# Transposing tiles 4 to 7 on VectorE instead of TensorE, spreading the scales of four tiles by one product, and one more gate and up piece ahead of the third attention unit

## The chip, the cores and the metric

The kernel runs on one core of a Trainium2 chip. A core has TensorE (matrix products, PE in the profile), VectorE (DVE), ScalarE (ACT), GpSimd (POOL) and SyncE (SP), which here only issues the DMAs. Each engine works through its own instructions in the order in which they were written, and waits for others by semaphores. The metric is the device time of one execution in microseconds.

## The reference

```python
xn = layernorm(x)                                 # x: 2048 rows of 640
qkv = xn @ wqkv                                   # 32 heads of 20
# each row attends to 8 rows: itself and those 2, 4, ... 14 rows back
logits = einsum("bhsd,bhswd->bhsw", q, k[idx]) * 20 ** -0.5   # masked where idx < 0
s = einsum("bhsw,bhswd->bhsd", softmax(logits), v[idx]) @ wo
h = (xn @ w_gate) * (xn @ w_up)                   # 640 -> 1536
out = x + s * silu(h @ w_down)                    # 1536 -> 640
```

All is in float32. The kernel writes each factor of a product as a high part (TensorE's rounded format) and a low part (the rest), and computes three products: high by high, high by low and low by high.

## The kernel before, in words

The 2048 rows stand as 16 tiles of 128 rows. Partition p of a tile holds row 16p + j of the sequence; tiles 0 to 7 are the even columns j ("even tiles"), tiles 8 to 15 the odd ones. Rows that attend to one another are of the same parity, so attention runs in units (g, r): six groups g of five or six heads by the two parities r, twelve units in all. Unit u multiplies its eight tiles by the weights of its group (`qkv(u, i)`, 15 products for tile i), ScalarE copies the result into q and kv, and the DMA shifts kv by one partition to fill the front. `attention(u)` is a generator of VectorE steps, which `advance` draws from a list `running` at a pace: each product stage adds to a credit, and each step takes its estimated length from it. So VectorE's attention of one unit is woven by hand into the product stages of the next ones. The kv buffers are two, one for each parity; unit u + 2 writes the one that attention(u) read.

The gate and up products run in pieces: `gate_up(f, ch)` is slice f of twelve slices of the hidden features, by chunk ch of four chunks of four tiles. A piece is a g half and a u half, of 15 products with 512 columns each. ScalarE copies g to gs, and the product hs = u * gs is made by `finish` in one of two ways: while an attention is running, by VectorE, deferred into the following piece or unit; otherwise by a copy on ScalarE and a product on GpSimd, at once. hs is stored to h_scr. From the third unit on, three or four pieces follow each unit (`piece`, the loop at L741); those that are left follow the last unit. Then come the last two slices, the output projection and the down projection with the gate.

Every product needs the normalized rows transposed, as four chunks of four tiles (`xT`, high and low part). This is made in two ways:

- Even tiles (0 to 7) go through TensorE. `norm` takes a tile's statistics on VectorE (`moments`), makes the inverse deviation (`rstd`) and applies shift and scale (L209). `trans` transposes it by five products with the identity (L223); ScalarE copies the high part (L224), VectorE subtracts it from the product for the low part (L225).
- Odd tiles (8 to 15) go through VectorE. Their statistics are taken from a first load of the rows. Then the tile is loaded again (`load_xq`) in another order, in which a 32 by 32 block transpose on VectorE (L253) gives the full transpose. In that order a partition holds pieces of four different rows, so the row's scales are needed in the partitions of other quarters: `spread` makes four products of the scales with selecting matrices `sel` (L240) and ScalarE copies the result (L241). `trans_odd` applies four shifts of 160 columns, transposes, lets ScalarE make the high part (L256), and makes the low part of the tile before (`low_parts`, L258), so that VectorE does not stand for ScalarE.

The first unit and the first slices have no attention to be woven with. Their order is written out from L635 to L710: TensorE does qkv(0, 0) to (0, 3) and the first half of piece (0, 0), the transposes of tiles 4 to 7 around piece (1, 0), qkv(0, 4) and (0, 5), piece (0, 1) with the spread in its middle, qkv(0, 6) and (0, 7), piece (1, 1), the eight qkv of unit 1, pieces (0, 2) to (1, 3), then unit 2.

Of the kernel before, what the change touches and what calls it, by code (L numbers as in the profile page):

```python
# [13 lines left out]
AF = mybir.ActivationFunctionType  # L14
# [20 lines left out]
QB = 32  # L35
NQ = P // QB
QC = D // NQ
# [13 lines left out]
def kernel(  # L51
# [11 lines left out]
    nc = tc.nc  # L63
# [66 lines left out]
    xt = {}  # L130
# [14 lines left out]
    xc = st([P, NE, D], "xc", NCH)  # L145
# [6 lines left out]
    ident = st([P, P], "ident", 1)  # L152
# [27 lines left out]
    def moments(s0, n, mv=None):  # L180
        stats = st([P, n, 2, 6], "stats", 2)
        mv = st([P, n, 2], "mv", 2) if mv is None else mv
        for i in range(n):
            for a in range(2):
                nc.vector.bn_stats(stats[:, i, a, :], xt[s0 + i][:, a * HALF:(a + 1) * HALF])
            nc.vector.bn_aggr(mv[:, i, :], stats[:, i])
        return mv
# [20 lines left out]
    def apply(y, m, r):  # L208
        nc.vector.tensor_scalar(y, y, m, r, op0=ALU.subtract, op1=ALU.mult)  # L209

    def norm(s0, n, mv=None):
        mv = moments(s0, n) if mv is None else mv
        r = st([P, n], "r", 2)
        rstd(mv[:, :, 1], r, n)
        for i in range(n):
            apply(xt[s0 + i], mv[:, i, 0:1], r[:, i:i + 1])

    def trans(s, bank=("q", 4)):
        hi, lo = xT_tile(s)
        for k0, k1 in ((0, 4), (4, KD)):  # L220
            p = pt([P, k1 - k0, P], *(("q", 4) if k0 else bank))
            for k in range(k0, k1):
                nc.tensor.transpose(p[:, k - k0, :], xt[s][:, k * P:(k + 1) * P], ident)  # L223
            nc.scalar.activation(hi[:, k0:k1, :], p, AF.Copy)  # L224
            nc.vector.tensor_sub(lo[:, k0:k1, :], p, hi[:, k0:k1, :].bitcast(F32))  # L225

    mvo = st([P, NE, 2], "mvo", 1)
    mro = st([P, 2, NE], "mro", 1)  # L230
    mrq = st([P, NQ, 2, NE], "mrq", 1)

    def load_xq(s, n, t):
        nc.sync.dma_start(t, xq[:, s - NE:s - NE + n, :])

    def spread():

        p = pt([P, NQ, 2, NE], "q", 4)
        for a in range(NQ):
            nc.tensor.matmul(p[:, a], sel[:, a], mro, start=True, stop=True)  # L240
        nc.scalar.activation(mrq, p, AF.Copy)  # L241

    halves = []

    def low_parts():
        while halves:
            halves.pop(0)()

    def trans_odd(s):
        for a in range(NQ):  # L250
            apply(xt[s][:, a * QC:(a + 1) * QC], mrq[:, a, 0, s - NE:s - NE + 1], mrq[:, a, 1, s - NE:s - NE + 1])
        y = st([P, KD, P], "ot", 2)
        nc.vector.transpose(y.rearrange("p k (q i) -> p k q i", i=QB),  # L253
                            xt[s].rearrange("p (q k j) -> p k q j", q=NQ, j=QB))
        hi, lo = xT_tile(s)
        nc.scalar.activation(hi, y, AF.Copy)  # L256
        low_parts()
        halves.append(lambda: nc.vector.tensor_sub(lo, y, hi.bitcast(F32)))  # L258


    UN = [(g, r) for g in range(len(GROUPS)) for r in range(DIL)]
# [21 lines left out]
    def qkv(u, i, runs=ALL_RUNS, at=None, act=None):  # L283

        g, r = UN[u]
        c = GROUPS[g] * DH
        p = pt([P, 3 * c], "q", 4)
        t0 = (i % TPC) * P
        for n, (a, b, k) in enumerate(runs):
            if n == at:  # L290
                act()
            nc.tensor.matmul(p, xT[(r * NE + i) // TPC][a][:, k, t0:t0 + P], wq[g][b][:, k], start=n == 0,  # L292
                             stop=n == len(runs) - 1, skip_group_check=act is not None)
        nc.scalar.activation(kv_t[u][:, :, W - 1 + i, :], p[:, c:].rearrange("p (a c) -> p a c", a=2), AF.Copy)  # L294
# [71 lines left out]
    running = []  # L366
# [14 lines left out]
    def gate_up_half(f, ch, n, p, c=slice(0, CH), **parts):  # L381
        mm3(p[:, c], [([t[:, k, n, :] for t in wf[f]], [t[:, k, c] for t in xT[ch]]) for k in range(KD)], **parts)

    def gate_up(f, ch, between=(), amid=(), part=None):
        if part is None:
            pp = [pt([P, CH], "g", 2), pt([P, CH], "u", 2)]
            c = slice(0, CH)
        else:
            pp, c = part, slice(CH // 2, CH)
        gate_up_half(f, ch, 0, pp[0], c)  # L390
        for act in amid:
            act()
        gs = st([P, CH], "gs", 2)
        nc.scalar.activation(gs, pp[0], AF.Copy)  # L394
        for act in between:
            act()
        share = (c.stop - c.start) / CH
        finish_piece()
        advance(PACE * 3.25 * share)
        gate_up_half(f, ch, 1, pp[1], c)  # L400

        def finish():
            hs = st([P, CH], "hs", 2)
            if running:
                nc.vector.tensor_mul(hs, pp[1], gs)  # L405
            else:
                nc.scalar.activation(hs, pp[1], AF.Copy)
                nc.gpsimd.tensor_mul(hs, hs, gs)
# [10 lines left out]
    def finish_piece():  # L419

        while unfinished:
            unfinished.pop(0)()
# [238 lines left out]
    sel = st([P, NQ, P], "sel", 1)  # L661
    nc.gpsimd.tensor_copy(sel.rearrange("p q (b i) -> p q b i", i=QB),
                          ident.rearrange("p (q i) -> p q i", i=QB).unsqueeze(2).to_broadcast([P, NQ, NQ, QB]))
# [8 lines left out]
    moments(10, 2, mvo[:, 2:4])  # L672
    load_xq(8, 4, xc[:, 4:8])
    trans(7)
    load_wf(2)
    qkv(0, 4)
    qkv(0, 5)
    moments(12, 2, mvo[:, 4:6])
    moments(14, 2, mvo[:, 6:8])
    load_xq(12, 3, xa)  # L680
    load_xq(15, 1, xd)
    nc.vector.tensor_copy(mro[:, 0, :], mvo[:, :, 0])
    rstd(mvo[:, :, 1], mro[:, 1, :], NE)
    gate_up(0, 1, amid=(spread,))
    trans_odd(8)
    trans_odd(9)
    qkv(0, 6)
    trans_odd(10)
    qkv(0, 7)
    trans_odd(11)  # L690
    gate_up(1, 1, amid=(lambda: trans_odd(12),))
    trans_odd(13)
    begin_unit(1)
    for i in range(8):
        if i == 3:
            running.append((0, attention(0)))
        if i == 2:
            load_wq(1, ((0, 3), (3, 5)))
            low_parts()
        if i < 2:  # L700
            trans_odd(14 + i)
# [12 lines left out]
    def piece():  # L714
        f, ch = pieces.pop(0)
        if ch == 0:
            load_wf(f + 1)
        gate_up(f, ch, (lambda: split_wf(f + 1, nc.gpsimd),) if ch == 1 else ())
# [19 lines left out]
            split_wq(UN[u + 1][0], nc.gpsimd)  # L738

    f0, f1 = KF - 2, KF - 1  # L740
    for u in range(2, len(UN)):  # L741
        unit(u)
        for _ in range(3 + (u in (2, 5)) if u + 1 < len(UN) else len(pieces)):
            if len(pieces) == 1:
                load_wf(f1)
            piece()
    for ch in range(NCH):
        gate_up(f0, ch)
        if ch == 0:
# [3 lines left out]
            t = load_wo((4,))  # L753
# [49 lines left out]
    for m in range(n_prod):  # L803
        n, j = divmod(m, 7)
# [61 lines left out]
```

## Time and profile before

| | us |
|---|---|
| median of 3 runs | 786.98 (786.91 to 787.13) |
| profiled execution | 786.92 |
| its span, first to last instruction | 785.0 |
| TensorE busy | 777.6 (99%) |
| VectorE busy | 661.4 (84%) |
| ScalarE busy | 234.4 (30%) |
| GpSimd busy | 145.5 (19%) |

A row of the profile's timeline gives the start, the time to the end of the last of a run of equal instructions, engine, line, operation, the tile written and those read, shape and count; in brackets is the idle time of the engine ahead of it and what ended that. Products overlap in the pipe, so a row's end lies behind the start of the next row. A row of the waits names the engine and line that waited, what it waited for, the total, how often, and the longest. Line numbers are those of the kernel before.

### The profile page before, as it was taken

To read this page: it belongs to the slowest core of one execution; us is meant where nothing else is said; L and a number is where in the kernel's file an instruction comes from. 1 tells how busy PE (TensorE), PEld (TensorE's weight loads), DVE (VectorE), ACT (ScalarE), POOL (GpSimd) and SP (SyncE) were. 2 spreads that over 40 slices of the span, in tenths; PEclk is the share of its full clock that TensorE was granted. 3 is DMA by queue.
4 is the path that set the end of the run, shared out by engine and by line. 5 is a ranking of instruction groups with operands and counts; after the bars stand their busy time and mean duration, and the time that the engine had idled before them with its cause. 6 is when DMAs were issued, how large, how long until landed. Compare 5 with 4: busy or idle time off the path is not lost.

```text
span 785.0 us, 11221 instructions
## 1 busy us (share of the span) xinstructions
PE 777.6 (99%) x4454; PEld 709.0 (90%) x4454; DVE 661.4 (84%) x660; ACT 234.4 (30%) x536; POOL 145.5 (19%) x110
## 2 busy tenths in 40 slices
PE   8999999999999999999999999999999999999997
PEld 6889898889898898899898989888899999999997
DVE  6989899999999979997999999991278677777775
ACT  4434211121122211311221212012366564444442
POOL 4401212022023100500231000113467600000000
PEclk9999999999999999999999999999999999999999
DMA  9162122141142221404032132332797574555534
GB/s 326 70 223 86 31 70 63 48 123 48 50 113 80 75 71 61 118 27 112 28 113 77 58 86 59 112 96 66 166 262 222 169 268 139 206 201 181 181 101 135
DMA packets 81661, 92.68 MB, mean 118 GB/s; under 512 B 23032, under 2 KB 63304, under 8 KB 81480
## 3 DMA queue, kind: packets, MB, share of 16 engines
q1 hardware_dynamic: 81608, 91.96, 37.9%
q8 instruction: 35, 0.57, 0.3%
q14 instruction: 18, 0.15, 0.1%
HBM read 54.53 MB, written 28.31 MB: 106 GB/s over the span
## 4 chain that ended last, share of the span: by engine, by line
PE 98%; ACT 1%; DMA 1%; DVE 0%; SPq 0%; issue 0%
PE q L292 27%; PE u L95 21%; PE g L95 21%; PE q L605 11%; PE q L95 9%; PE u L605 5%; PE g L605 3%; DMA wraw<-in_wqkv 1%; PE q L223 0%; ACT wf L85 0%; ACT xc L224 0%; SPq L135 0%; DVE t L209 0%; ACT wqh L85 0%; PE q L240 0%
## 5 line engine op out<-in xcount | busy, mean ns | idle before, releaser
L95 PE MATMUL u<-xc,wf 128*128 128x512 f32 (+1 forms) x735 | 176.2, 391 | 0.0
L95 PE MATMUL g<-xc,wf 128*128 128x512 f32 (+1 forms) x735 | 176.2, 391 | 0.0
L95 PEld LDWEIGHTS u<-xc,wf 128*128 128x128 f32 x735 | 135.9, 188 | 32.1
L95 PEld LDWEIGHTS g<-xc,wf 128*128 128x128 f32 x735 | 135.4, 188 | 30.8
L292 PE MATMUL q<-wqh,xc 128*128 128x300 f32 (+1 forms) x960 | 159.8, 310 | 0.9 <-ACT xc L224 0.9
L292 PEld LDWEIGHTS q<-wqh,xc 128*128 128x128 f32 x960 | 146.1, 188 | 2.9 <-ACT xc L224 1.3
L326 DVE TENSOR_TENSOR t<-q,kv 128x1600 f32<-128x1600 f32 (+1 forms) x48 | 98.8, 2058 | 9.6 <-DMA kv<-kv 9.6
L347 DVE TENSOR_TENSOR t<-e,kv 128x1600 f32<-128x1600 f32 (+1 forms) x48 | 96.9, 2037 | 1.1
L86 POOL TENSOR_TENSOR wf<-wraw,wf 128x256 fp32r<-128x256 f32 (+2 forms) x22 | 47.1, 2161 | 253.0 <-ACT wf L85 253.0
L329 DVE TENSOR_REDUCE lg<-t 128x80 f32<-128x1600 f32 (+1 forms) x48 | 92.6, 1930 | 1.2
L394 ACT ACTIVATE gs<-g 128x512 f32<-128x512 f32 x48 | 28.7, 598 | 205.8 <-PE g L95 197.2
L292 PE MATMUL q<-wql,xc 128*128 128x300 f32 (+1 forms) x480 | 86.3, 310 | 0.0
L355 DVE TENSOR_TENSOR t<-t,t 128x1600 f32<-128x1600 f32 (+1 forms) x36 | 78.6, 2184 | 1.1
L292 PEld LDWEIGHTS q<-wql,xc 128*128 128x128 f32 x480 | 74.4, 188 | 0.0
L294 ACT ACTIVATE kv<-q 128x200 f32<-128x200 f32 (+1 forms) x96 | 33.4, 348 | 135.7 <-PE q L292 135.6
L605 PE MATMUL q<-xc,wf 128*128 128x320 f32 x432 | 67.3, 309 | 0.0
L605 PEld LDWEIGHTS q<-xc,wf 128*128 128x128 f32 x432 | 64.3, 188 | 0.0
L86 POOL TENSOR_TENSOR wql<-wraw,wqh 128x300 fp32r<-128x300 f32 (+4 forms) x15 | 33.2, 2239 | 142.5 <-ACT wqh L85 142.5
L95 PE MATMUL q<-wf,wf 128*128 128x320 f32 x156 | 35.7, 311 | 0.0
L405 DVE TENSOR_TENSOR hs<-u,gs 128x512 f32<-128x512 f32 x39 | 26.6, 683 | 0.8 <-issue 0.8
L86 DVE TENSOR_TENSOR wf<-ot,wf 128x640 fp32r<-128x640 f32 x13 | 17.2, 1322 | 12.0 <-ACT wf L85 12.0
L95 PEld LDWEIGHTS q<-wf,wf 128*128 128x128 f32 x156 | 26.1, 189 | 0.0
(169 smaller groups left out, 890.8 us busy)
## 6 DMA issues: line engine op xcount, KB each, us to landing
h_scr<-hs SPq DMA_DIRECT2D x48, 256.0 KB, 2.3
wraw<-in_wgu SPq DMA_DIRECT2D x12, 640.0 KB, 4.9
t<-h_scr SPq DMA_DIRECT2D x8, 768.0 KB, 7.5
hs<-s_scr SPq DMA_DIRECT2D x16, 320.0 KB, 4.0
gs<-in_x SPq DMA_DIRECT2D x16, 320.0 KB, 4.4
wraw<-h_scr SPq DMA_DIRECT2D x12, 384.0 KB, 5.7
out<-q SPq DMA_DIRECT2D x14, 320.0 KB, 3.6
wraw<-in_wd SPq DMA_DIRECT2D x12, 320.0 KB, 4.9
```

Source lines behind the costliest of these rows:

```text
L86: eng.tensor_sub(lo, raw, hi.bitcast(F32))
L95: nc.tensor.matmul(acc, a, b, start=first and n == 0, stop=last and n == len(runs) - 1)
L292: nc.tensor.matmul(p, xT[(r * NE + i) // TPC][a][:, k, t0:t0 + P], wq[g][b][:, k], start=n == 0, stop=n == len(runs) - 1, skip_group_check ...
L294: nc.scalar.activation(kv_t[u][:, :, W - 1 + i, :], p[:, c:].rearrange("p (a c) -> p a c", a=2), AF.Copy)
L326: nc.vector.tensor_mul(t, q.rearrange("p i c -> p (i c)").unsqueeze(1).to_broadcast([P, 2, NE * c]), places(0, j))
L329: nc.vector.tensor_reduce(out=lg[:, :, j:j + 2].rearrange("p n a -> p a n"), in_=heads(t), op=ALU.add, axis=AX.X)
L347: nc.vector.tensor_mul(heads(t), pw, heads(places(1, j)))
L355: nc.vector.tensor_add(acc, acc, t)
L394: nc.scalar.activation(gs, pp[0], AF.Copy)
L405: nc.vector.tensor_mul(hs, pp[1], gs)
L605: nc.tensor.matmul(p, y[:, i, k], wd_t[name][k][:, l], start=new and r == 0, stop=r == len(runs) - 1, skip_group_check=True)
```

## The change

Tiles 4 to 7 are now treated as the odd tiles are: statistics from the first load, a second load of each tile in the other order, four shifts, the block transpose on VectorE, high part on ScalarE, low part on VectorE. `trans_q` replaces `trans_odd`, and works by groups of four tiles. The host's array xq holds twelve tiles instead of eight. The twenty transposing products of these tiles on TensorE are gone; those of tiles 0 to 3 remain.

`scales(s0)` makes the scales of a group and multiplies them by `quarter`, a matrix of ones and zeros, so that each partition's two numbers per tile stand only in the columns of its own quarter. `spread(s0)` is then one product with one selecting matrix, for each of three groups; before it was four products for all eight odd tiles. GpSimd builds `quarter` and `sel` in ten small steps.

The written order changes with it. qkv(0, 4) to (0, 7) now run in a row behind piece (1, 0). Statistics of tiles 8 to 15 come behind the transposes of 4 to 7. Piece (0, 2) stands in the middle of unit 1, and attention(0) is put on the list behind it and behind the last transpose. Piece (2, 0) runs ahead of unit 2, so two pieces instead of three are left behind the last unit. hs is made by VectorE, deferred, in all pieces but the very last.

```diff
-    def spread():
-        p = pt([P, NQ, 2, NE], "q", 4)
-        for a in range(NQ):
-            nc.tensor.matmul(p[:, a], sel[:, a], mro, start=True, stop=True)
-        nc.scalar.activation(mrq, p, AF.Copy)
+    def scales(s0):
+        mv, mr = stat[s0]
+        nc.vector.tensor_copy(mr[:, 0, :], mv[:, :, 0])
+        rstd(mv[:, :, 1], mr[:, 1, :], TPC)
+        own[s0] = st([P, NQ, 2, TPC], "own", 2)
+        nc.vector.tensor_mul(own[s0], mr.unsqueeze(1).to_broadcast([P, NQ, 2, TPC]),
+                             quarter.unsqueeze(2).unsqueeze(3).to_broadcast([P, NQ, 2, TPC]))
+    def spread(s0):
+        p = pt([P, NQ, 2, TPC], "q", 4)
+        nc.tensor.matmul(p, sel, own[s0], start=True, stop=True)
+        spread_t[s0] = st([P, NQ, 2, TPC], "mrq", 2)
+        nc.scalar.activation(spread_t[s0], p, AF.Copy)
...
+        last = (f, ch) == (KF - 1, NCH - 1)
...
-            if running:
+            if not last:
                 nc.vector.tensor_mul(hs, pp[1], gs)
...
-        if not running:
+        if last:
             finish_piece()
...
-    norm(4, 4)
+    quarter, sel = st([P, NQ], "quarter", 1), st([P, P], "sel", 1)
...
+    for i in range(TPC):
+        moments_q(4 + i, 1)
+        load_xq(4 + i, 1, xc[:, i:i + 1])
+    scales(4)
     qkv(0, 2)
     qkv(0, 3)
     gate_up(0, 0, part=part0)
-    trans(4)
-    trans(5)
-    moments(8, 2, mvo[:, 0:2])
-    gate_up(1, 0, amid=(lambda: trans(6),))
...
+    spread(4)
+    trans_q(4)
+    finish_piece()
+    trans_q(5)
+    gate_up(1, 0)
     load_wf(2)
+    trans_q(6)
+    trans_q(7)
     qkv(0, 4)
     qkv(0, 5)
...
+    low_parts()
+    finish_piece()
+    moments_q(8, 4)
+    load_xq(8, 4, xc[:, 4:8])
+    scales(8)
+    qkv(0, 6)
+    qkv(0, 7)
+    moments_q(12, 4)
     load_xq(12, 3, xa)
     load_xq(15, 1, xd)
...
+    scales(12)
+    gate_up(0, 1, amid=(lambda: spread(8),))
+    trans_q(8)
+    trans_q(9)
+    finish_piece()
+    trans_q(10)
+    gate_up(1, 1, amid=(lambda: spread(12),))
+    trans_q(11)
     begin_unit(1)
+    trans_q(12)
+    finish_piece()
+    for i in range(TPC):
+        if i == 1:
             load_wq(1, ((0, 3), (3, 5)))
+        qkv(1, i)
+    trans_q(13)
+    trans_q(14)
+    gate_up(0, 2)
+    trans_q(15)
+    low_parts()
+    running.append((0, attention(0)))
+    for i in range(TPC, NE):
         qkv(1, i)
         advance(PACE * 1.9)
     running.append((1, attention(1)))
     split_wq(1, nc.gpsimd)
-    gate_up(0, 2)
     gate_up(1, 2)
...
+    piece()
     for u in range(2, len(UN)):
         unit(u)
...
-    odd = arrays["x"].reshape(NQ, QB, NE, DIL, NQ, QC)[:, :, :, 1]
-    arrays["xq"] = lay(odd.transpose(3, 1, 2, 0, 4).reshape(P, NE, D))
+    quarters = arrays["x"].reshape(NQ, QB, NE, DIL, NQ, QC).transpose(3, 4, 1, 2, 0, 5).reshape(DIL, P, NE, D)
+    arrays["xq"] = lay(np.concatenate([quarters[0][:, TPC:], quarters[1]], axis=1))
```

More of the change, by code (lines that the diff above doesn't have):

```diff
@@ L225, in trans, with moments_q, trans_q @@
             nc.vector.tensor_sub(lo[:, k0:k1, :], p, hi[:, k0:k1, :].bitcast(F32))
-    mvo = st([P, NE, 2], "mvo", 1)
-    mro = st([P, 2, NE], "mro", 1)
-    mrq = st([P, NQ, 2, NE], "mrq", 1)
-    def load_xq(s, n, t):
-        nc.sync.dma_start(t, xq[:, s - NE:s - NE + n, :])
-    def spread():
-        p = pt([P, NQ, 2, NE], "q", 4)
-        for a in range(NQ):
[L240 to L249, printed above, removed]
-        for a in range(NQ):
-            apply(xt[s][:, a * QC:(a + 1) * QC], mrq[:, a, 0, s - NE:s - NE + 1], mrq[:, a, 1, s - NE:s - NE + 1])
+    stat = {s: (st([P, TPC, 2], "mvo", 3), st([P, 2, TPC], "mro", 3)) for s in range(TPC, NT, TPC)}
+    own, spread_t = {}, {}
+    def moments_q(s, n):
+        s0 = s // TPC * TPC
+        moments(s, n, stat[s0][0][:, s - s0:s - s0 + n])
+    def load_xq(s, n, t):
+        nc.sync.dma_start(t, xq[:, s - TPC:s - TPC + n, :])
+    def scales(s0):
[10 more added lines that the diff above has]
+        nc.scalar.activation(spread_t[s0], p, AF.Copy)
+    halves = []
+    def trans_q(s):
+        m, i = spread_t[s // TPC * TPC], s % TPC
+        for a in range(NQ):
+            apply(xt[s][:, a * QC:(a + 1) * QC], m[:, a, 0, i:i + 1], m[:, a, 1, i:i + 1])
         y = st([P, KD, P], "ot", 2)
```

37 lines of the change are left out of this document (11 added, 26 removed).

## The prediction

> **What bounds the kernel now.** I read the page's busy shares and its chain first, then who TensorE waited for.
>
> ```profile
> span 785.0 us, 11221 instructions
> ...
> PE 777.6 (99%) x4454; PEld 709.0 (90%) x4454; DVE 661.4 (84%) x660; ACT 234.4 (30%) x536; POOL 145.5 (19%) x110
> ...
> PE 98%; ACT 1%; DMA 1%; DVE 0%; SPq 0%; issue 0%
> ```
> ```profile
> PE q L292 <- ACT xc L224: 0.9, 2, 0.6
> PE q L223 <- PE u L95: 0.4, 1, 0.4
> ```
>
> TensorE is busy 99% of the span, carries 98% of the chain, and behind its first products waits for nothing longer than 0.6 us. So a product taken from it is worth its whole time, as long as no new wait appears, and VectorE, at 84%, is the engine that could bring one. The stage that changes, on TensorE in order of time (start, us, what, count):
>
> ```profile
> 22.93 1.92 PE L95 MATMUL g<-xc,wf 128*128 128x256 f32 x15
> 24.68 1.91 PE L95 MATMUL u<-xc,wf 128*128 128x256 f32 x15
> 26.96 1.30 PE L223 MATMUL q<-ident,xc 128*128 128x128 f32 x10 [0.37 <-PE u L95]
> 28.02 3.75 PE L95 MATMUL g<-xc,wf 128*128 128x512 f32 x15
> 31.61 0.71 PE L223 MATMUL q<-ident,xc 128*128 128x128 f32 x5
> ...
> 36.11 0.94 PE L292 MATMUL q<-wqh,xc 128*128 128x300 f32 x5
> ...
> 43.81 0.96 PE L240 MATMUL q<-mro,sel 128*128 128x16 f32 x8
> 44.62 3.74 PE L95 MATMUL u<-xc,wf 128*128 128x512 f32 x15
> ...
> 59.31 0.86 PE L292 MATMUL q<-wqh,xc 128*128 128x300 f32 x5
> ...
> 75.81 3.66 PE L95 MATMUL g<-xc,wf 128*128 128x512 f32 x15
> 79.30 3.66 PE L95 MATMUL u<-xc,wf 128*128 128x512 f32 x15
> ```
>
> Products overlap, so I count from start to start. From 59.31 to 75.81 run eight products of qkv: 2.06 us each. A half of gate_up (15 products of 512 columns) is 79.30 − 75.81 = 3.49 us, a piece 7.0; a half of 256 columns is 24.68 − 22.93 = 1.75.
>
> **What the change takes from TensorE and gives it.** Before, 36.11 − 24.68 = 11.43 us go from the u half of piece (0, 0) to qkv(0, 4), and hold 1.75 + 7.0 of that half and piece (1, 0). The other 2.68 us are the twenty transposes of tiles 4 to 7 with the 0.37 us wait ahead of them. They go. The spread of the odd tiles is four products; from 36.11 to 59.31 there are 23.20 us, of which 4 × 2.06 and four halves make 22.24, so it costs 0.96. In its place come three spreads of one product each: by a quarter of that row 0.24 each; bounds 0.10 (an eighth of 0.81) and 0.96. I take 0.24, as a product of the same kind.
>
> So TensorE saves 2.68 + 0.96 − 3 × 0.24 = 2.92 us, less the waits it gets anew. These stand in VectorE's queue.
>
> ```profile
> 20.31 0.88 DVE L185 BATCH_NORM_STATS2 stats<-xc 128x6 f32<-128x320 f32 x2
> ...
> 24.44 0.34 DVE L194 TENSOR_SCALAR rstd<-mv 128x4 f32<-128x4 f32 x1
> ...
> 41.90 0.17 DVE L682 COPY mro<-mvo 128x8 f32<-128x8 f32 x1
> ...
> 43.14 0.17 DVE L206 TENSOR_TENSOR mro<-rstd 128x8 f32<-128x8 f32 x1
> ...
> 49.65 1.45 DVE L258 TENSOR_TENSOR xc<-ot,xc 128x640 fp32r<-128x640 f32 x1 [0.44 <-ACT xc L256]
> 51.03 1.17 DVE L209 TENSOR_SCALAR xc<-xc,mrq 128x160 f32<-128x160 f32 x4
> ...
> 53.00 0.78 DVE L258 TENSOR_TENSOR xc<-ot,xc 128x640 fp32r<-128x640 f32 x1
> 53.71 1.17 DVE L209 TENSOR_SCALAR xc<-xc,mrq 128x160 f32<-128x160 f32 x4
> ...
> 68.85 1.82 DVE L326 TENSOR_TENSOR t<-q,kv 128x1600 f32<-128x1600 f32 x1
> ...
> 88.98 0.49 DVE L340 TENSOR_REDUCE sm<-e 128x40 f32<-128x320 f32 x1 [3.35 <-ACT e L338]
> ...
> 104.51 0.68 DVE L405 TENSOR_TENSOR hs<-u,gs 128x512 f32<-128x512 f32 x1
> 105.11 1.81 DVE L355 TENSOR_TENSOR t<-t,t 128x1600 f32<-128x1600 f32 x1
> ```
> ```profile
> 44.80 0.22 ACT L241 ACTIVATE mrq<-q 128x64 f32<-128x64 f32 x1 [2.54 <-PE q L240]
> ...
> 53.12 0.74 ACT L256 ACTIVATE xc<-ot 128x640 fp32r<-128x640 f32 x1 [2.17 <-DVE ot L253]
> ...
> 86.56 0.60 ACT L394 ACTIVATE gs<-g 128x512 f32<-128x512 f32 x1 [6.40 <-PE g L95]
> ...
> 106.06 0.34 ACT L294 ACTIVATE kv<-q 128x200 f32<-128x200 f32 x1 [4.91 <-PE q L292]
> ```
> ```profile
> 25.18 0.60 POOL L662 COPY sel<-ident 128x512 f32<-128x512 f32 x1
> ...
> 49.12 1.30 POOL L408 TENSOR_TENSOR hs<-hs,gs 128x512 f32<-128x512 f32 x1 [11.30 <-ACT hs L407]
> ```
>
> The steps from these rows: statistics of four tiles 24.44 − 20.31 = 4.1; scales of a group 43.14 + 0.17 − 41.90 = 1.4 plus 0.2 for the new product of 32 columns (bounds 0.17 and 0.34, the nearest small rows), so 1.6; shift and transpose of a tile, 53.00 − 51.03 = 1.97; a low part 0.71; ScalarE's high part 0.74 in between; a product hs 105.11 − 104.51 = 0.60.
>
> **The first spread.** VectorE reaches scales(4) at 24.44, as now, and has its operand at about 26.5. GpSimd builds sel in five fills, three sums and a copy instead of one copy, from 25.18: at least 0.8 us (nine times about 0.09), at most 3.5 (each step at 0.60 or less, fills at a tenth). By the columns it is about 1.3, so 26.5. TensorE is free at 24.68 + 1.75 = 26.43. I take the spread at 26.88, a wait of 0.45 (from 0.05 to 2.3, where sel is the last).
>
> **The chain on VectorE.** With the spread's copy on ScalarE (0.22, some 0.3 after the product starts), VectorE starts on tile 4 at 27.6. Its order is: tile 4, hs, tile 5, low 4, tile 6, low 5, tile 7, low 6, low 7, hs, statistics of 8 to 11, scales, statistics of 12 to 15, scales, tiles 8 and 9, low 8, hs, tile 10, low 9, tile 11, low 10, tile 12, low 11. Summed, low 4 ends at 32.85, low 5 at 35.5, low 6 at 38.2, low 7 at 39.0, the scales of 8 at 45.3 and of 12 at 51.1, low 8 at 55.7, low 9 at 59.0, low 10 at 61.7, low 11 at 64.35.
>
> TensorE: spread done 27.12, piece (1, 0) to 34.12, qkv(0, 4) to (0, 7) to 42.36, g of (0, 1) to 45.86, spread(8), u to 49.60, g of (1, 1) to 53.10, spread(12), u to 56.84, then qkv(1, 0) to (1, 3) at 56.84, 58.90, 60.96 and 63.02. A product of qkv reads the low part in its last third, 1.37 us after its start: 58.2, 60.3, 62.3, 64.4. So low 8 has 2.5 us to spare, low 9 1.3, low 10 0.6, and **low 11 nothing**. Each us that VectorE is later from here back to tile 4 is a us of TensorE. I put 0.2 us there.
>
> Sum: 2.92 − 0.45 − 0.2 = 2.27 us.
>
> **What lies beside.** Four hs of this stage and four near the end leave ScalarE and GpSimd for VectorE; three are in the chain (1.8 us). Four reloads of 320 KB, 1.28 MB more to move, go into SP's queue right behind the last first load, each after its tile's statistics (from 21.3), with only the later h_scr stores behind them. SP then holds load_wf(2), two shift DMAs of kv (waiting for qkv(0, 4)), a store, and only then the reload of 8 to 11, which waits for the statistics of tile 11 (43.6), and behind it the second pair of kv shifts.
>
> ```profile
> xc<-in_xq SPq DMA_DIRECT2D x1, 1280.0 KB, 6.8
> t<-in_xq SPq DMA_DIRECT2D x1, 960.0 KB, 9.8
> ```
> ```profile
> DMA  9999999977744310000000000000000000000000
> ```
>
> At 6.8 us it lands at 50.4, wanted at 51.1: covered, by 0.7. The second row is the DMA share from 20 to 27 us in 40 slices: the engines run empty at 22.8, so tile 4's reload, wanted at 27.5, has 6.2 us and a free path.
>
> **Attention and the piece moved ahead.** attention(0) starts at about 73.8 instead of 68.85, five us late. Its exponentials stand on ScalarE behind a gs, now that of (0, 3), whose g ends at 65.08 + 7.0 + 8.25 + 7.0 + 3.5 = 90.8. From the gs at 86.56 to VectorE's next step at 88.98 it was 2.4; so that step now runs at 93.2. Its last read of kv ends where the row at 104.51 begins, so at 108.7. Unit 2 writes the same kv buffer: its first copy ran at 106.06, 1.5 us behind. With piece (2, 0) ahead, TensorE starts unit 2 at 63.02 + 2.06 + 7.0 + 8.25 + 28 = 108.3, and the copy comes at 110.5: 1.8 us to spare, as before. The piece itself costs nothing, being work moved from behind the last unit. Without this cover the copy would wait 5.2 us, which the three further product banks (6.2 us) would just hold. load_wf(3) moves ahead with the piece and waits in SP for GpSimd's low half of wf(2), holding back only stores. At the end, attention(11) finishes later by about five us, against this wait:
>
> ```profile
> DVE ot L466 <- DMA wraw<-o_scr: 20.9, 1, 20.9
> ```
>
> **A rule weighed.** The low part at 49.65 took 1.45, the one at 53.00 0.78; GpSimd's hs product, at 49.12 for 1.30, ends when the first gets going. With the hs products gone from GpSimd, all low parts of the chain should take the short value, which the sum uses. The Trainium skill, "SBUF — State Buffer", section "SBUF: two separate sides", says VectorE and GpSimd share a port pair by an exclusive lock, held for a whole instruction; the trace agrees (0.67 us lost). By that rule, the other side also holds: GpSimd's new small steps and the fill of the second kv buffer now fall on the scales of tile 4 and its first shift.
>
> ```profile
> 61.55 1.26 POOL L278 MEMSET kv<- 1x1400 f32 x1
> ```
>
> **The rivals.**
> 1. *Tiles 8 to 11 land late.* At the 9.8 us of the other reload, 53.4 instead of 51.1: the chain is 2.3 later and so is low 11. 787.0, no change. For it: kv shifts share the path. Against: the neighbours that filled the engines then (load_wf(2), two more reloads) are now earlier or later. 0.13.
> 2. *GpSimd delays the start.* If its fill of 1.26 us holds up tile 4's first shift, the whole chain is 1.26 later, and low 11 with it: 784.65 + 1.26 = 785.9, within 0.2%. For it: the fill stands right behind sel in GpSimd's queue. Against: half of it may be over by 27.6. 0.05. (This is the time by the rule of the section just named.)
> 3. *Slower: VectorE becomes the bound of the stage.* Its 36.8 us from tile 4 to low 11 have no slack, so TensorE pays each us. It decides at 2.27 us (6% of the chain), and costs 0.2% from 3.84; were all eight low parts at 1.45, it would be 8 × 0.67 = 5.4 us: 790.1. For it: the mean share of 84% hides that this stretch is full, and rows beside GpSimd are slow. Against: GpSimd is idle there. 0.10.
> 4. *Slower by the first reload.* Were tile 4's reload as slow as the first loads of single tiles (the row below), it would land at 21.3 + 11.8 = 33.1, the chain 5.6 later: 790.2. Against: the empty engines above. 0.08.
>
> ```profile
> t<-in_x SPq DMA_DIRECT2D x3, 320.0 KB, 11.8
> ```
>
> **The numbers.** The profiled execution took 786.92 us, 1.92 outside its span of 785.0, and the median of the runs is 786.98. 786.92 − 2.27 = 784.65, against the median 784.7. The forecast has the remaining 0.64, its own range 783.6 (first spread without wait, spreads at 0.10) to 785.4. For four in five the range is 783.7 to 787.6, which takes in rivals 1 and 2 and sel as the last, and leaves out 3 and 4. 0.2% of 787 is 1.57 us, about what can be told from no change: faster 0.64, same 0.18, slower 0.18.
>
> **What would show it.** Right: no L223 row on xc; qkv(0, 4) at about 34.1, qkv(1, 0) at 56.8; attention(0) at 73.8 on VectorE; spreads of about 0.24; TensorE's waits up by under 0.7 us. Wrong: a wait of qkv in unit 1 for VectorE's low parts over 1 us, a wait at the first spread for GpSimd, or VectorE waiting for a reload.

## The result and the profile after

| | us |
|---|---|
| median of 22 runs after the change | 785.87 (785.35 to 786.74) |
| median of 22 runs before it | 787.31 (786.82 to 788.47) |
| ratio of after to before | 0.9983, 95% interval 0.9976 to 0.9989 |
| profiled execution after | 786.40, its span 784.6 |

The change saves 1.3 us (0.9 to 1.9), 0.17%. That is in the forecast direction, some 60% of the 2.27 us forecast, and just inside the 0.2% that the prediction called no change. The page of the changed kernel, busy shares and the chain's share by engine:

```profile
PE 776.7 (99%) x4432; PEld 708.3 (90%) x4432; DVE 667.5 (85%) x691; ACT 230.6 (29%) x527; POOL 135.6 (17%) x110
...
PE 96%; DMA 1%; POOL 1%; DVE 1%; SPq 0%; ACT 0%; issue 0%
```

TensorE has 22 instructions fewer and is still the bound. Of its waits behind its first products, the 0.4 us ahead of the transposes are gone, and the changed stage has one new wait, that for `sel` at the first spread:

```profile
PE q L250 <- POOL sel L681: 0.5, 1, 0.5
```

Another new one, of 0.5 us for rows that VectorE normalizes (L209), lies in the start-up at 17.27, ahead of the change. The stage on TensorE (timeline, as in the prediction; the five rows that carry the steps):

```profile
25.51 1.94 PE L95 MATMUL u<-xc,wf 128*128 128x256 f32 x15
27.99 0.41 PE L250 MATMUL q<-own,sel 128*128 128x32 f32 x2 [0.55 <-POOL sel L681]
...
35.31 0.85 PE L304 MATMUL q<-wqh,xc 128*128 128x300 f32 x5
...
58.04 0.85 PE L304 MATMUL q<-wqh,xc 128*128 128x300 f32 x5
...
109.75 0.85 PE L304 MATMUL q<-wqh,xc 128*128 128x300 f32 x5
```

From the u half of piece (0, 0) to qkv(0, 4) it is now 35.31 − 25.51 = 9.80 us (11.43 before), and from there to qkv(1, 0) 58.04 − 35.31 = 22.73 (23.20 before). Together 2.10 us are saved of the 2.47 forecast for these two stretches. Unit 1 and pieces (0, 2) to (1, 3) take 109.75 − 58.04, less 7.0 for the piece ahead, 44.71 us; before, they took 103.97 − 59.48 = 44.49 (first two rows of the next fence). 0.2 us are lost there, and the stage as a whole brings 1.9 us.

More is lost behind the stage, where nothing was changed. Units of the chain (start, us, what), before and then after:

```profile
59.48 16.49 PE q L292 x120
103.97 16.48 PE q L292 x120
...
343.08 19.84 PE q L292 x120
```
```profile
109.91 16.59 PE q L304 x120
...
349.39 19.84 PE q L304 x120
```

A unit of five heads (products of 300 columns) takes 16.59 instead of 16.48 us, 138.25 ns a product instead of 137.3; one of six heads takes 19.84 as before. Eight units of five heads make 8 × 0.11 = 0.9 us, six of them (0.66) behind the stage. 1.9 − 0.66 = 1.2 us, which is the measured gain within its interval. The profiled executions differ by only 786.92 − 786.40 = 0.5 us, because the one of the changed kernel comes to its u half at 25.51 us instead of 24.68. The start-up varies from run to run: the kernel before with its weights moved (an experiment below) comes there at 25.29, and a variant of the changed kernel at 24.82.

VectorE, GpSimd and ScalarE, where the prediction had named moments:

```profile
26.74 0.26 DVE L244 TENSOR_TENSOR own<-mro,quarter 128x32 f32<-128x32 f32 x1
28.67 1.37 DVE L209 TENSOR_SCALAR xc<-xc,mrq 128x160 f32<-128x160 f32 x4 [1.67 <-ACT mrq L252]
...
64.84 0.78 DVE L266 TENSOR_TENSOR xc<-ot,xc 128x640 fp32r<-128x640 f32 x1
...
75.10 1.82 DVE L338 TENSOR_TENSOR t<-q,kv 128x1600 f32<-128x1600 f32 x1
...
96.39 4.45 DVE L359 TENSOR_TENSOR t<-e,kv 128x1600 f32<-128x1600 f32 x1
...
109.27 1.81 DVE L359 TENSOR_TENSOR t<-e,kv 128x1600 f32<-128x1600 f32 x1
```
```profile
26.00 0.09 POOL L675 MEMSET quarter<- 128x4 f32 x1
...
27.68 0.26 POOL L681 COPY sel<-sel 128x96 f32<-128x96 f32 x1
27.88 1.25 POOL L290 MEMSET kv<- 1x1400 f32 x1
...
96.18 2.98 POOL L86 TENSOR_TENSOR wf<-wraw,wf 128x1280 fp32r<-128x1280 f32 x1 [6.47 <-ACT wf L85]
```

VectorE has its operand `own` at 27.0, `sel` is there only at 27.94. Low part 11 starts at 64.84, short (0.78) like all of the chain (predicted 64.35 as its end, with a start-up 0.8 us earlier). The last read of kv ends at 111.08. The 4.45 us stand beside a GpSimd split of weights that runs from 96.18 to 99.16, and the same product takes 1.81 elsewhere. The kernel before has such a slow product in the same stretch, too, also beside a split (97.19 to 101.05):

```profile
98.25 4.48 DVE L355 TENSOR_TENSOR t<-t,t 128x1600 f32<-128x1600 f32 x1
```

### The profile page after: what moved, and what is told of

Its sections match the earlier page's. It is cut to its first block, busy times and chain, and to the rows that moved or that the text cites. A ratio compares the mean times of both kernels' runs of the same rounds, so it can differ in the third digit from the quotient of the medians.

```text
span 784.6 us, 11205 instructions
## 1 busy us (share of the span) xinstructions
PE 776.7 (99%) x4432; PEld 708.3 (90%) x4432; DVE 667.5 (85%) x691; ACT 230.6 (29%) x527; POOL 135.6 (17%) x110
## 4 chain that ended last, share of the span: by engine, by line
PE 96%; DMA 1%; POOL 1%; DVE 1%; SPq 0%; ACT 0%; issue 0%
PE q L304 26%; PE u L95 21%; PE g L95 21%; PE q L618 11%; PE q L95 9%; PE u L618 5%; PE g L618 3%; DMA t<-in_xb 1%; POOL wf L86 0%; SPq L106 0%; DVE stats L185 0%; SPq L135 0%; POOL kv L290 0%; DVE t L209 0%; ACT xc L224 0%
## 5 line engine op out<-in xcount | busy, mean ns | idle before, releaser
L338 DVE TENSOR_TENSOR t<-q,kv 128x1600 f32<-128x1600 f32 (+1 forms) x48 | 97.0, 2021 | 9.0 <-DMA kv<-kv 9.0
L86 POOL TENSOR_TENSOR wf<-wraw,wf 128x256 fp32r<-128x256 f32 (+2 forms) x22 | 44.6, 2043 | 282.3 <-ACT wf L85 282.3
L367 DVE TENSOR_TENSOR t<-t,t 128x1600 f32<-128x1600 f32 (+1 forms) x36 | 75.3, 2091 | 1.0
L86 POOL TENSOR_TENSOR wql<-wraw,wqh 128x300 fp32r<-128x300 f32 (+4 forms) x15 | 36.0, 2423 | 170.0 <-ACT wqh L85 170.0
L418 DVE TENSOR_TENSOR hs<-u,gs 128x512 f32<-128x512 f32 x47 | 32.1, 683 | 10.3 <-PE u L95 9.5
```

The source lines that it names most:

```text
L86: eng.tensor_sub(lo, raw, hi.bitcast(F32))
L338: nc.vector.tensor_mul(t, q.rearrange("p i c -> p (i c)").unsqueeze(1).to_broadcast([P, 2, NE * c]), places(0, j))
L367: nc.vector.tensor_add(acc, acc, t)
```

## The experiments

### Where the missing 0.9 us went: the place of the tiles in SBUF

The changed kernel's small tiles (statistics, scales, sel) have other sizes and orders, and so everything allocated behind them lies elsewhere: the high part of the qkv weights begins 96 bytes above a multiple of 256 instead of 32, the gate and up weights have moved by the same 192 bytes. One theory: products of 300 columns depend on that place. The rival: VectorE's or GpSimd's new load slows them. An unused tile puts the weights back:

```diff
     eps_t = st([P, 1], "eps", 1)
+    st([P, 48], "pad", 1)
```

> The changed kernel with an unused 192-byte tile ahead of the statistics, so that the attention weights wqh and wql lie at the byte addresses that they have in the kernel before (120352 and 127552, 32 and 64 modulo 128; in the changed kernel 120160 and 127360, 96 and 0). Nothing else differs. Theory A (addresses): a product of 300 columns reads 1200 bytes of a weight slice in each partition, and costs more where the slice's address modulo 128 is above 80, so that it reaches into an eleventh piece of 128 bytes; that holds for 3 of the 15 products of a tile in the kernel before and 5 of 15 in the changed one. Start to start, the products of units 2 to 7 come back from 138.25 to 137.35 ns, and as units 0 to 7 hold 960 of them, the time falls by 0.8 to 0.9 us against the changed kernel: ratio to the kernel before about 0.9972. Rival (the 0.9 ns come from the order of the work, such as VectorE's busier queue or the transfers beside): 138.25 stays and the ratio stays at 0.9983.

785.05 us (784.63 to 785.40), ratio to before 0.9972 (0.9962 to 0.9983): 0.8 us better than the changed kernel, with the same instructions. Its chain:

```profile
109.60 16.48 PE q L305 x120
```

The reverse moves the weights of the kernel before to the new kernel's place within 256 bytes, with the unused tile at the same spot:

```diff
     eps_t = st([P, 1], "eps", 1)
+    st([P, 16], "pad", 1)
```

> The kernel before with an unused 64-byte tile ahead of the statistics, so that the weights lie at 96 and 0 modulo 128 as in the changed kernel. Theory A: the products of 300 columns take 138.25 ns start to start instead of 137.35, and the kernel is 0.8 to 0.9 us slower than before: ratio 1.0011. Rival (order of the work): 137.35 and ratio 1.0000.

787.73 us, ratio 1.0008 (0.9999 to 1.0016), with the slow rate:

```profile
60.09 16.59 PE q L293 x120
```

Both ways agree: the place alone decides between 16.48 and 16.59 us a unit, and it costs the change 0.8 us that no step of its own costs. The unused tile moves every tile that is allocated behind it, the weights among them, so these two runs don't show which of the tiles counts; a later run shows that the place of the qkv weights isn't the whole of it.

A place between the two was to show the rule behind it (`st([P, 8], "pad", 1)` at the same spot in the kernel before):

> The kernel before with an unused 32-byte tile, so that wqh lies at 64 and wql at 96 modulo 128. By the count of slices above 80 modulo 128 it is 2 of 5 for wql (used once for each tile) and 1 of 5 for wqh (used twice): 4 of 15 products, so 137.8 ns start to start, half way between. If another rule of the address holds (64 bytes, say), the mean is that of one of the two others.

A single run, 790.7 us. The first unit in the chain takes 16.62 us (at a granted clock of 1.00), where the count of slices gave 137.8 × 120 = 16.54, so a simple count of slices that cross some boundary falls. Something else showed: the halves of gate and up pieces, whose weights now begin on a multiple of 128 bytes, take 3.40 us instead of 3.50, and yet the kernel is slower, since TensorE now waits:

```profile
PE u L95 <- DVE hs L406: 5.5, 4, 2.3
```

To part the two, the gate and up weights of the kernel before, with what is allocated behind them, were moved by 32 bytes, the qkv weights, q and kv left in place:

```diff
+    st([P, 8], "pad", 1)
     split_wf(0, nc.gpsimd, range(KD + 1))
```

> Before with an unused 32-byte tile taken ahead of the first gate and up weights: those weights now begin on a multiple of 128 bytes, the qkv weights, q and kv stay where they were. In the run where everything from the qkv weights on was moved by 32 bytes, a gate or up half took 3.40 us instead of 3.50 and VectorE's attention products took 2061 and 1999 ns instead of 1925 and 1896, and the time was no better. Theory: the faster halves come from the place of the gate and up weights, VectorE's slower products from the place of q and kv; then here halves of 3.40 us, VectorE's products near 1925 and 1896 ns, and of the 1394 x 5.4 ns = 7.5 us only what VectorE's chain in units 2 to 5 lets through: between 782 and 786 us. Rival: VectorE's products are slower because TensorE is faster; then products above 2000 ns again, waits of TensorE for hs, and 787 to 791 us. Third: the halves stay at 3.50 us, since another tile's place made them shorter; then 787.0 to 787.6 us.

The median is 789.35 us, ratio 1.0022 (1.0009 to 1.0034): slower. The profiled execution is by far the quickest of its twelve (784.71; the others took 787.94 to 790.77), and even there TensorE waits:

```profile
245.86 3.40 PE g L95 x15
```
```profile
PE u L95 <- DVE hs L405: 3.4, 3, 1.4
```

The shorter halves do come from the place of the gate and up weights: of what a half reads, the transposed rows were allocated ahead of the unused tile and stayed where they were. But in the median nothing is kept of the time they free. In the profiled execution VectorE is late with hs, and TensorE waits for it; that the slower executions lost their time in the same way is likely, but no trace shows it. Of VectorE's slower products in the run before, those of q by k (five heads) are back at 1925 ns while those of e by v stay at 1995, so neither the theory nor the rival is right for both. The outcome is the rival's.

### The wait at the first spread

In the changed kernel `sel` is late. Here `quarter` and `sel` are built at the very start (with an unused tile of 96 bytes that keeps the weights where they were within 128 bytes):

```diff
     eps_t = st([P, 1], "eps", 1)
+    st([P, 24], "pad", 1)
     nc.vector.memset(eps_t, EPS)
+    quarter, sel = st([P, NQ], "quarter", 1), st([P, P], "sel", 1)
+    nc.gpsimd.memset(quarter, 0.0)
...
-    quarter, sel = st([P, NQ], "quarter", 1), st([P, P], "sel", 1)
-    nc.gpsimd.memset(quarter, 0.0)
...
```

> The changed kernel with GpSimd's ten steps for quarter and sel put right behind the identity matrix at the start, where GpSimd is idle, and a 96-byte tile that keeps the weights at 96 and 0 modulo 128. Theory: TensorE's wait for sel at the first spread (0.55 us in the profile of the changed kernel, 0.73 from start to start) goes; VectorE's chain starts as much earlier, so no wait takes its place, and the time falls by 0.5 to 0.7 us against the changed kernel: ratio about 0.9975. Rival (VectorE's operand is as late as sel): the wait turns into one for VectorE's own, of more than 0.3 us, and the gain is under 0.3 us.

786.27 us, ratio 0.9985 (0.9976 to 0.9994): no gain. TensorE's wait was handed to another engine, and the rows of VectorE and GpSimd say why:

```profile
PE q L260 <- DVE own L254: 0.4, 1, 0.4
```
```profile
25.31 0.16 DVE L214 TENSOR_TENSOR rstd<-rstd 128x4 f32<-128x4 f32 x1
25.50 1.02 DVE L215 TENSOR_SCALAR rstd<-rstd 128x4 f32<-128x4 f32 x1
```
```profile
25.23 1.26 POOL L300 MEMSET kv<- 1x1400 f32 x1
```

With `sel` out of the way, GpSimd's fill of the second kv buffer moves forward and now lies on VectorE's scales: an operation on 4 columns with one input takes 1.02 us instead of 0.17 and ends when the fill ends (26.5). The Trainium skill, "SBUF — State Buffer", section "SBUF: two separate sides", describes this as a lock on a shared port pair, held for a whole instruction; the 0.85 us lost agree. Besides, a unit takes 16.65 us here: the weights are at yet another place within 256 bytes, although at the same one within 128.

The same without the unused tile, so with the qkv weights' high part on a multiple of 128 bytes:

> As the run with sel built early, without the pad: wqh lies at 0, wql at 32, and the gate and up weights wf at 64 modulo 128 (at 32 in the changed kernel, 96 before, 0 in the run where a half of gate and up took 3.40 instead of 3.50 us). If what counts for wf is whether it lies on 64 bytes, its halves take 3.40; if 128 bytes, 3.50. For wqh I have no rule that held so far: between 137.3 and 138.8 ns. Time: 0.2 us less than the changed kernel from the earlier sel if wf stays at 3.50, and up to 9 us less on TensorE if it goes to 3.40, of which VectorE may let through only a part.

785.19 us, ratio 0.9975 (0.9965 to 0.9985), a unit 16.54 us, halves 3.50. Most of what the profiled execution gains over that of the run before (785.25 against 785.75 us) is the products': units of five heads take 0.11 us less, those of six, at 19.89 instead of 19.79, 0.1 more. The medians differ by more (1.1 us), which the profiles do not show. The wait for `own` is still there (0.6 us).

If the fill is what holds VectorE, both fills should go where GpSimd idles, between the splits of the first two gate and up columns (here with an unused tile of 32 bytes ahead of `quarter` and `sel`):

```diff
+    zero_front(0)
+    begin_unit(1)
     split_wf(1, nc.gpsimd, range(KD + 1))
-    zero_front(0)
...
     trans_q(11)
-    begin_unit(1)
     trans_q(12)
```

> After with sel and quarter built at the start and both fills of kv's first rows put between the splits of the first two gate and up columns, where GpSimd idles for 4 us; the qkv weights begin as before's do (32 bytes above a multiple of 128). Theory: the fill was what held VectorE's short operation (1.02 us in place of 0.17) when sel was early; now it takes 0.17 us, own is ready about 0.8 us sooner, TensorE waits under 0.1 us at the first spread, products of 300 columns take 137.4 ns: 784.4 to 784.9 us. Rival: the fills, now between 16 and 19 us, hold VectorE in the work for tiles 2 and 3, and the start gives back what the spread gains: 785.0 to 785.5 us.

The mechanism holds, the time does not: it is outside both ranges. The operation is short again and TensorE does not wait at the spread:

```profile
25.69 0.17 DVE L215 TENSOR_SCALAR rstd<-rstd 128x4 f32<-128x4 f32 x1
```
```profile
24.97 1.94 PE L95 MATMUL u<-xc,wf 128*128 128x256 f32 x15
26.75 0.30 PE L260 MATMUL q<-own,sel 128*128 128x32 f32 x2
```

But 786.05 us, ratio 0.9989 (0.9980 to 0.9997). The start is not to blame. A unit takes 16.55 us and a half 3.51 to 3.52 instead of 3.50, although the weights lie as those of the kernel before within 128 bytes. With the gate and up weights 32 bytes further on, as in the run on the kernel before:

> The run before this one with the unused 32-byte tile ahead of the first gate and up weights as well, so that these begin on a multiple of 128 bytes. Theory: halves of 3.40 us; as the changed kernel's VectorE has little to spare in units 2 to 5, part of the 7.5 us is lost to waits for hs: 779 to 784 us. Rival: VectorE's products grow with it and TensorE waits for hs for more than the halves save: 785 to 789 us.

784.17 us, ratio 0.9960 (0.9947 to 0.9973). The halves are 3.49 us, not 3.40, so neither the theory nor the rival foresaw it rightly: being on a multiple of 128 bytes is not enough. By the order of allocation the qkv weights lie where they lay in the run before, and so do the transposed rows, yet units of five heads, 16.55 us there, now alternate between two times (even units, then odd ones):

```profile
108.56 16.64 PE q L314 x120
153.10 16.56 PE q L314 x120
```

So the place of a product's own operands does not decide its rate alone.

The last run keeps the early `sel` and fills, and moves everything from the statistics to the mask by exactly 512 bytes against the run with the weights put back; what lies behind stays exactly where it was there. The edit, shown against the first run with both fills early:

```diff
-    st([P, 8], "pad", 1)
+    st([P, 40], "pad", 1)
...
     mask = st([1, NE, W], "mask", 1)
+    st([P, 8], "pad2", 1)
```

> The run with sel and the fills early once more, its tiles placed anew: everything from the moments to the mask lies exactly 512 bytes above its place in the changed kernel with the weights back, and everything behind it exactly where it lay there. Theory: products go at one rate wherever the tiles keep their distance and their place within 512 bytes; then 300 columns take 137.3 ns and 512 columns 233.5 again, TensorE does not wait at the first spread, which starts 0.7 us sooner than in the changed kernel, and the time is 0.6 to 0.8 us below that of the changed kernel with the weights back, which was 785.05: 784.2 to 784.5 us. Rival: the rate hangs on more than the place within 512 bytes (on which engine works at the same time, or on the whole address); then the rates move by up to 1 ns either way as in the run before, 0.9 us for the 960 products of 300 columns and 1.4 us for the 1394 of 512: 783.5 to 786.5 us.

783.62 us (783.59 to 784.26), ratio 0.9954 (0.9940 to 0.9967), the best of all, and the rates are back:

```profile
108.55 16.48 PE q L314 x120
```

Unit 2 starts 109.60 − 108.55 = 1.05 us sooner than with late `sel`, for the same start-up (u half at 25.22 against 25.17). Of this, 0.78 us lie between the u half and the first spread (1.75 instead of 2.53), and 0.21 in the first four products of unit 1 (8.29 instead of 8.50), which wait less for VectorE's low parts. The theory had counted only the first, and its range begins 0.6 us above the measured median. That the rates hold it foresaw rightly, for the one step of 512 bytes that was tried; which places are good, and which tiles count, stays open.

### Is VectorE's chain without slack?

Two idle operations were put on VectorE behind `scales(12)`:

```diff
     scales(12)
+    junk = st([P, 1600], "junk", 1)
+    nc.vector.memset(junk, 1.0)
+    nc.vector.tensor_mul(junk, junk, junk)
```

> The changed kernel with two VectorE instructions on 1600 columns of an unused tile (a fill and a product) behind the scales of tiles 12 to 15, so that VectorE is some 2.5 to 3.5 us late from tile 8 on (their durations are to be read in the trace). If VectorE's chain has no slack, as predicted, TensorE waits for low parts 9 to 11 by what is added less at most 0.6, and the time rises by that: 2 to 3 us. Rival (the chain has slack that the count missed, or another engine sets the stage): under 1 us.

789.37 us, ratio 1.0028 (1.0018 to 1.0039), 3.5 us above the changed kernel.

```profile
52.52 1.39 DVE L712 MEMSET junk<- 128x1600 f32 x1 [0.28 <-issue]
53.94 1.83 DVE L713 TENSOR_TENSOR junk<-junk 128x1600 f32<-128x1600 f32 x1
```
```profile
PE q L304 <- DVE xc L266: 1.9, 4, 0.9
...
PE q L304 <- ACT xc L264: 0.5, 1, 0.5
```

The chain on VectorE is 1.39 + 1.83 + 0.28 = 3.5 us later, and TensorE, waiting for the high and low parts, reaches its last half ahead of unit 2 at 109.67 instead of 106.25: 3.4 us, of which the view of the waits names 2.4. Nothing is absorbed, where the expectation allowed for up to 0.6.

### What making hs on VectorE is worth

The old way of finishing a piece (VectorE while an attention runs, else ScalarE and GpSimd):

```diff
-            if not last:
+            if running:
...
-        if last:
+        if not running:
             finish_piece()
```

> The changed kernel with the products hs made as before: by ScalarE and GpSimd, at once, while no attention runs. VectorE loses three products of 0.60 us in the chain from tile 4 to low 11, and GpSimd gains four of 1.3. Theory: the rule of the shared port costs about as much as is saved, each GpSimd product holding one VectorE instruction by up to 0.7 us; low 11 is no later than 1 us earlier, and as TensorE waits only some 0.1 us there, the ratio stays at 0.9983 within 0.05%. Rival (the hs products matter): low 11 is over 1 us earlier or later and the time moves by 0.5 us or more.

787.86 us, ratio 1.0008 (0.9999 to 1.0017): 2.0 us above the changed kernel, the whole gain gone. Shifts of a tile take 1.17 us and a low part 0.78; those beside GpSimd's hs, and one beside its fill of kv, do not:

```profile
28.30 1.69 DVE L209 TENSOR_SCALAR xc<-xc,mrq 128x160 f32<-128x160 f32 x4 [1.67 <-ACT mrq L252]
...
36.13 2.15 DVE L209 TENSOR_SCALAR xc<-xc,mrq 128x160 f32<-128x160 f32 x4
...
52.07 2.18 DVE L209 TENSOR_SCALAR xc<-xc,mrq 128x160 f32<-128x160 f32 x4
...
62.36 1.34 DVE L266 TENSOR_TENSOR xc<-ot,xc 128x640 fp32r<-128x640 f32 x1
63.63 1.51 DVE L209 TENSOR_SCALAR t<-t,mrq 128x160 f32<-128x160 f32 x4
```
```profile
27.79 1.28 POOL L421 TENSOR_TENSOR hs<-hs,gs 128x512 f32<-128x512 f32 x1 [0.21 <-ACT hs L420]
35.82 1.54 POOL L421 TENSOR_TENSOR hs<-hs,gs 128x512 f32<-128x512 f32 x1 [6.75 <-ACT hs L420]
...
52.04 1.29 POOL L421 TENSOR_TENSOR hs<-hs,gs 128x512 f32<-128x512 f32 x1 [14.68 <-ACT hs L420]
61.72 1.30 POOL L421 TENSOR_TENSOR hs<-hs,gs 128x512 f32<-128x512 f32 x1 [8.39 <-issue]
62.96 1.26 POOL L290 MEMSET kv<- 1x1400 f32 x1
```

Three hs products of 0.60 us that VectorE no longer makes are less than what the collisions cost it: against the changed kernel, whose first shift takes 1.37, these five rows lose 0.32 + 0.98 + 1.01 + 0.56 + 0.34 = 3.2 us. Less the 1.8 saved, that is 1.4 us, and TensorE loses about as much: from the u half to unit 2 it takes 110.85 − 25.14 = 85.71 us, and 109.75 − 25.51 = 84.24 in the changed kernel. The view of the waits names 1.1 of this 1.5, for low parts. The other 0.5 us between the medians are not in this stage, and no run shows their cause.

### The piece ahead of unit 2

```diff
     f0, f1 = KF - 2, KF - 1
-    piece()
     for u in range(2, len(UN)):
```

> The changed kernel without piece (2, 0) ahead of unit 2 (it comes behind unit 2, and three pieces are left behind the last unit). My theory (the prediction's): unit 2 starts 7 us earlier on TensorE, at about 102.7; its first copy into kv on ScalarE then waits some 4 to 5 us for the last read of attention(0), the four product banks hold that, and TensorE waits for nothing or under 0.5 us; the ratio stays within 0.1% of the changed kernel's 0.9983. Rival (the piece is what makes the change pay): TensorE waits 2 us or more in unit 2 and the time rises by as much, ratio 1.001 or above.

788.29 us (787.85 to 789.02), ratio 1.0013 (1.0005 to 1.0022): 2.4 us above the changed kernel, and slower than before the change.

```profile
110.15 0.34 ACT L306 ACTIVATE kv<-q 128x200 f32<-128x200 f32 x1 [10.60 <-DVE t L359]
```
```profile
178.01 4.45 DVE L367 TENSOR_TENSOR t<-t,t 128x1600 f32<-128x1600 f32 x1
```
```profile
102.20 0.85 PE L304 MATMUL q<-wqh,xc 128*128 128x300 f32 x5
...
144.03 3.76 PE L95 MATMUL u<-xc,wf 128*128 128x512 f32 x15 [0.29 <-DVE hs L418]
...
183.12 3.76 PE L95 MATMUL u<-xc,wf 128*128 128x512 f32 x15 [1.25 <-DVE hs L418]
186.72 0.85 PE L304 MATMUL q<-wqh,xc 128*128 128x300 f32 x5
```

The same unit 4 in the changed kernel:

```profile
191.91 0.85 PE L304 MATMUL q<-wqh,xc 128*128 128x300 f32 x5
```

ScalarE's first copy of unit 2 stands for kv until 110.15, over 5 us late (5.2 by the prediction), and TensorE loses only 0.3 us in that unit: the product banks nearly hold. The loss is later. TensorE is 7 us further ahead of VectorE's attention from here on, and stands for hs at 144 us and again around 183, where a VectorE product beside a GpSimd split takes 4.45 us instead of 1.82 and the hs behind it is late. From unit 2 to unit 4 TensorE takes 186.72 − 102.20 = 84.52 us, and 191.91 − 109.75 = 82.16 in the changed kernel: 2.4 us, which is the difference of the medians. (The profiled spans, 786.4 and 784.6, differ by only 1.8, because this execution comes to its u half at 24.97, the changed kernel's at 25.51.)

## Why the prediction was right or wrong

- **What goes from TensorE (2.68 us) and the odd tiles' spread (0.96): right.** Between qkv(0, 4) and qkv(1, 0), 0.47 us were saved where 0.96 − 0.48 was forecast. Up to qkv(0, 4) it was 11.43 − 9.80 = 1.63 of a forecast 1.99.
- **The first spread: the term "a wait of 0.45" was mis-sized.** TensorE was free at 25.51 + 1.75 = 27.26 and began the spread at 27.99: 0.73 us. That it would be `sel` was foreseen as the upper branch. GpSimd began the steps (nine by the trace, not ten) when foreseen (26.00, which is 25.18 and the 0.8 us of the slower start-up), but they took 27.94 − 26.00 = 1.94 us, not the 1.3 that the number of columns had given. With `sel` and both fills early the wait is gone, and the kernel gains on the run with the weights put back: 1.4 us between the medians (785.05 to 783.62), 1.05 at the start of unit 2 in the profiles. A wait at the first spread for GpSimd was also one of the signs of being wrong that the prediction had named.
- **VectorE's chain has nothing to spare at low 11: right.** Two added operations of 3.5 us cost 3.5 us. The term of 0.2 us stood for the 0.2 lost over unit 1 and its pieces, half of which is the slower products there (8 × 2.07 instead of 8 × 2.06 us); the other 0.1 are lost ahead of piece (0, 2), among the products that read low 8 to 11.
- **"All low parts of the chain should take the short value": right,** 0.78 in each, and this is what the change lives on: with hs left on GpSimd the gain is gone. The hs change, which the prediction listed as work of 1.8 us added to the chain, is worth 2.0 us. Four more places agree with the lock that the Trainium skill, "SBUF — State Buffer", section "SBUF: two separate sides", describes: the scales (1.02 instead of 0.17, in the run with `sel` early), the shifts (2.15 instead of 1.17, beside GpSimd's hs), the first shift of the changed kernel (1.37 beside the fill from 27.88) and the attention's products (4.45 instead of 1.81).
- **"The piece itself costs nothing", without it the banks "would just hold": the banks did but for 0.3 us, the conclusion was wrong.** The step that failed is that unit 2's copy was taken as the only place where TensorE's lead shows: without the piece TensorE stands for hs behind unit 2, and the kernel loses 2.4 us. The cover was thinner than worked out, too: the last read ended at 111.08 instead of 108.7, and the first copy stood at 112.02, which leaves 0.9 us instead of 1.8. Of these 2.4 us of the read, 0.8 are the slower start-up, 0.9 the later start of attention(0) and of its step behind the exponentials (94.91 instead of 93.2), and 0.6 one more product hs on VectorE in the stretch behind that step. The product of 4.45 us is no part of it, as the row of the kernel before held one of 4.48.
- **The missing term: the place of the tiles, 0.8 us.** With the weights put back the kernel is 2.2 us faster than before (787.29 to 785.05), nearly the forecast. No step of the sum asked what else moves when small tiles change their sizes. It is the largest part of the miss: 2.27 − 0.28 (spread) − 0.66 (units 2 to 7 at the slower rate) leaves 1.33, the measured gain. Both errors go the same way, so none hid another. By the prediction's own limit of 1.57 us the outcome is "same", to which it gave 0.18, and not "faster" (0.64); the interval of the gain, 0.9 to 1.9 us, takes in that limit.
- **Rivals.** Neither reload was late: VectorE waits for none, and low 8 to 11 follow without a gap. GpSimd's fill cost the first shift 0.2 us, not 1.26, as only its last 0.46 us (28.67 to 29.13) lay on the shift. That it can fall on the scales instead, as the prediction said, the run with `sel` early shows (0.85 us). VectorE did not become the bound of the stage, but it is the next one: in the profiles of the two runs of the kernel before with shorter halves, and of the one without the piece ahead, TensorE stands for hs.

## What to carry to other kernels

When a change moves the sizes or the order of small tiles, compare the rate of products that it does not touch, a unit's time in the chain, before any other explanation; if it differs, put the tiles back with an unused one and measure again. Where an engine's chain sets the time of another, look at what a third engine runs beside it: here a fill of 1.26 us decided whether an earlier `sel` brought anything. A lead of the bounding engine over the next one is not free: ask at which later buffer it ends.

## What the runs showed of the hardware

- TensorE's rate depends on where tiles lie in SBUF. Products of 300 columns took 137.3 to 138.8 ns from start to start (units of 16.48 to 16.65 us), with the same instructions; those of 512 columns 226.7 to 234.7 (halves of 3.40 to 3.52). A shift by 512 bytes left the rates as they were. Shifts changed one or both: by 32 and 64 bytes in the kernel before, by 192 in the changed kernel, and by 384 (the first run with both fills early against the one with the weights put back). No rule that fits all of them was found, and with the qkv weights in the same place the rate still moved (16.55 to 16.64 us a unit) when the gate and up weights and what lies behind them moved by 32 bytes.
- A fill by GpSimd, which reads nothing, held a one-input operation of VectorE until its end (1.02 instead of 0.17 us), and let the two-input operation ahead of it, which began 0.08 us into the fill, run at 0.16.
